# A new order for the first batch of an attention-and-FFN kernel: k first, split roles for the k features, first FFN units 128 columns wide

## The chip, the cores and the metric

The kernel runs on one core of a Trainium2 chip. The metric is the time of one execution in microseconds (us); most executions of one kernel agree within 0.3%. In the text PE is the tensor engine, DVE is VectorE, ACT is ScalarE, POOL is GpSimd, SP is the engine whose queue issues most DMAs. The granted clock of PE is the share of its full clock that the profile shows as allowed.

## The reference

A linear attention with cosine and sine position weights, then a gated FFN. Cut to what matters:

```python
# q, k, v: (8, 8, 576, 64) = batch, heads, sequence, head size
r = maximum(x, 0); phi(x) = concat([r * cos_w, r * sin_w], axis=-1)
kv  = einsum('bhsf,bhsd->bhfd', phi(k), v)        # 128 x 64 per head
z   = sum(phi(k), axis=2)
out = einsum('bhsf,bhfd->bhsd', phi(q), kv) / (einsum('bhsf,bhf->bhs', phi(q), z) + 1e-6)
x   = out as (4608 tokens, 512)
y   = (gelu(x @ w_gate) * (x @ w_val)) @ w_out    # 512 -> 1536 -> 512
```

Nearly all the work is the FFN's matmuls. The attention of later batches is spread among them; only the first batch's attention has nothing to hide behind. That stretch, up to the first FFN matmul, is called the prologue here.

## The kernel before

Loads and the first batch, with cuts marked. One token row group is `(pair m, j)`: four head pairs, nine j, 64 numbers each. `kp` and `qp` are phi(k) and phi(q), `vx` is v in bf16 with a column of ones (so that z comes out of the same matmul as kv). `qT` is phi(q) transposed; the numerators are the matmuls of `qT` with kv; `den` and `rec` are the denominators and their reciprocals, `x_sb` the attention's output and `xT` its transpose; `gel` and `hT` are the gelu of the gate and its product with the value; `jt` counts the twelve blocks of 128 hidden units. Banks are parts of PSUM, the memory that PE writes.

```python
    load(nc.sync, "qf", q, 0, ((0, 2),), 0, 4)      # q, j 0 to 3 ("the q slice")
    load(nc.scalar, "qf", q, 0, ((2, 2),), 0, 4)
    load(nc.sync, "kf", k, 0, ((0, 2),))
    load(nc.scalar, "kf", k, 0, ((2, 2),))
    load(nc.sync, "vf", v, 0, ((0, 2),))
    load(nc.sync, "vf", v, 0, ((2, 1),))
    # ... tables of cos and sin
    load(nc.scalar, "vf", v, 0, ((3, 1),))
    load(nc.scalar, "qf", q, 0, ((0, NP),), 4, R)   # q, j 4 to 8 ("the rest of q")
    # ...
    def prep(name, b, j0, j1, m=0, n=NP, parts=(0, 1)):       # DVE, four pairs per op
        for j in range(j0, j1):
            for part in parts:
                nc.vector.tensor_scalar(dst[:, m:m + n, j, ...], src[:, m:m + n, j], 0.0,
                                        (cos_t, sin_t)[part][:, j:j + 1], op0=ALU.max, op1=ALU.mult)
    # prep_wide: DVE scalar_tensor_tensor, one pair, many j; prep_act: ACT Relu with a scale
    def kv_unit(b, groups=1):
        ps = psum[:, 4:6]                                     # both groups in the same banks
        # ...
        for g in range(groups):
            # 36 matmuls, then
            nc.scalar.copy(kv[:, g * per:(g + 1) * per], psv[:, g * per:(g + 1) * per])
    # ...
    nc.gpsimd.tensor_copy(probe, staged["kf", 0][:, 2, 0:1])  # POOL waits for k,
    load_w(0, 2)                                              # then issues all weight loads
    for jt in range(2, 8, 3):                                 # (on POOL's queue; they cast
        load_w(jt, 3)                                         # float32 to bf16 on the way)
    # ... loads of batch 1 and of w_out
    for m in range(NP):
        for part in range(2):
            prep_wide("qp", 0, 0, 4, m, part)
    turn_q_pe(0, 0, 4, (0, 1), (None, None))
    prep_act("kp", 0, 1, 0, 2)
    prep_wide("kp", 0, 0, R, 0, 0)
    prep_wide("kp", 0, 0, R, 1, 0)
    cast_v(0, 0, 2, nc.vector.tensor_copy)
    prep_act("kp", 0, 1, 2, 2)
    # ... the other two pairs the same way
    turn_copies(0, 0, 4, (0, 1), (nc.scalar.copy, nc.vector.tensor_copy))
    keep_warm(50)                  # 128x128 matmuls whose result nobody reads
    kv_unit(0, 2)
    keep_warm(8)
    nm_unit(0, 0)                  # numerators; then on DVE den, rec, x_sb = numerator * rec
    nm_unit(0, 1, 0)
    keep_warm(8)
    xt_unit(0, 0)                  # PE transposes, ACT copy to xT
    keep_warm(8)
    xt_unit(0, 1, 7)
    prep("qp", 0, 4, 6)
    prep("qp", 0, 6, 8)
    for jt in range(8):
        gv_unit(0, 256, jt)        # FFN: gate and value of 128 hidden units, 256 tokens
        # ... narrow turns of q (both in bank 7), numerators and transposes of tiles 2 to 4
```

Of the kernel before, what the change touches and what calls it, by code (L numbers as in the profile page):

```python
# [9 lines left out]
FP32 = mybir.dt.float32  # L10
# [6 lines left out]
def kernel(  # L17
# [14 lines left out]
    nc = tc.nc  # L32

    B, H, S, D = q.shape
# [5 lines left out]
    NP = H // 2  # L40
    R = S // 64
# [5 lines left out]
    consts = ctx.enter_context(tc.tile_pool(name="consts", bufs=1))  # L47
# [8 lines left out]


    psum = psp.tile([128, 8, BLK], FP32)
    ring = [0, 1, 2, 3]

    def next_bank():
        ring.append(ring.pop(0))
# [6 lines left out]
    staged = {}  # L69

    def load(eng, name, src, b, cuts=((0, NP),), j0=0, j1=R):
        if (name, b) not in staged:
            staged[name, b] = inp.tile(
                [128, NP, R * D], FP32, name=name, bufs=2 if name == "qf" else 1
            )
        js = slice(j0 * D, j1 * D)
        for m, n in cuts:
            eng.dma_start(
                out=staged[name, b][:, m:m + n, js], in_=rows(src, b)[:, m:m + n, js]
            )  # L80
# [8 lines left out]
    def load_w(jt0, n):  # L89
        sl = slice(jt0 * 128, (jt0 + n) * 128)  # L90
        nc.gpsimd.dma_start(out=wg_sb[:, :, sl], in_=wg_r[:, :, sl])
        nc.gpsimd.dma_start(out=wv_sb[:, :, sl], in_=wv_r[:, :, sl])
# [3 lines left out]



    load(nc.sync, "qf", q, 0, ((0, 2),), 0, 4)
    load(nc.scalar, "qf", q, 0, ((2, 2),), 0, 4)  # L100
    load(nc.sync, "kf", k, 0, ((0, 2),))
    load(nc.scalar, "kf", k, 0, ((2, 2),))
    load(nc.sync, "vf", v, 0, ((0, 2),))
    load(nc.sync, "vf", v, 0, ((2, 1),))

    pos_i = consts.tile([128, R], mybir.dt.int32)
    nc.gpsimd.iota(pos_i, pattern=[[1, R]], base=0, channel_multiplier=R)
# [2 lines left out]
    ident = consts.tile([128, 128], BF16)  # L110
# [10 lines left out]
    cos_t = consts.tile([128, R], FP32)  # L121
    nc.scalar.activation(sin_t, pos_f, AF.Sin, scale=th_scale)
    nc.scalar.activation(cos_t, pos_f, AF.Sin, scale=-th_scale, bias=half_pi)
    load(nc.scalar, "vf", v, 0, ((3, 1),))
    load(nc.scalar, "qf", q, 0, ((0, NP),), 4, R)
    warm = consts.tile([128, 1], FP32)
    nc.scalar.activation(warm, half_pi, AF.Gelu)
    vx_tiles = []
# [13 lines left out]
    def prep(name, b, j0, j1, m=0, n=NP, parts=(0, 1)):  # L142

        dst = phi_tile(name, b)
        src = staged[name[0] + "f", b].rearrange("p m (j d) -> p m j d", j=R)
        for j in range(j0, j1):
            for part in parts:
                nc.vector.tensor_scalar(  # L148
                    dst[:, m:m + n, j, part * D:(part + 1) * D],
                    src[:, m:m + n, j],  # L150
                    0.0,
                    (cos_t, sin_t)[part][:, j:j + 1],
                    op0=ALU.max,
                    op1=ALU.mult,
                )

    def prep_wide(name, b, j0, j1, m, part):
        nc.vector.scalar_tensor_tensor(  # L158
            phi_tile(name, b)[:, m, j0:j1, part * D:(part + 1) * D],
            staged[name[0] + "f", b][:, m].rearrange("p (j d) -> p j d", j=R)[:, j0:j1],  # L160
            0.0,
            (cos_t, sin_t)[part][:, j0:j1, None].to_broadcast([128, j1 - j0, D]),
            op0=ALU.max,
            op1=ALU.mult,
        )

    def prep_act(name, b, part, m=0, n=NP, j0=0, j1=R):

        dst = phi_tile(name, b)
        src = staged[name[0] + "f", b].rearrange("p m (j d) -> p m j d", j=R)  # L170
        for j in range(j0, j1):
            nc.scalar.activation(
                dst[:, m:m + n, j, part * D:(part + 1) * D],
                src[:, m:m + n, j],
                AF.Relu,
                scale=(cos_t, sin_t)[part][:, j:j + 1],
            )

    def cast_v(b, m=0, n=NP, copy=nc.gpsimd.tensor_copy):
        copy(  # L180
            vx_tiles[b % 2][:, m:m + n, :, 0:D],
            staged["vf", b][:, m:m + n].rearrange("p m (j d) -> p m j d", j=R),
        )
# [10 lines left out]
    def turn_q_pe(b, j0, n, banks=(4, 5), engines=None):  # L194

        if engines is None:
            engines = (nc.scalar.copy, nc.vector.tensor_copy)
        per = NP // len(banks)
        views = [
            psum[:, g].bitcast(BF16)[:, 0:per * n * 128].rearrange(  # L200
                "f (m j c) -> f m j c", m=per, j=n
            )
            for g in banks
        ]
        for m in range(NP):
            for j in range(n):
                nc.tensor.transpose(  # L207
                    out=views[m // per][:, m % per, j],
                    in_=phi["qp", b][:, m, j0 + j, :],
                    identity=ident,  # L210
                )
        if engines[0] is not None:
            turn_copies(b, j0, n, banks, engines)

    def turn_copies(b, j0, n, banks, engines):
        per = NP // len(banks)
        for g, copy in enumerate(engines):
            ps = psum[:, banks[g]].bitcast(BF16)[:, 0:per * n * 128].rearrange(
                "f (m j c) -> f m j c", m=per, j=n
            )  # L220
            for i in range(2):
                copy(
                    qt_tile(b)[i][
                        :, g * per:(g + 1) * per, j0 * 64:(j0 + n) * 64
                    ].rearrange("f m (j p) -> f m j p", p=64),
                    ps[:, :, :, i * 64:(i + 1) * 64],
                )

    def turn_q_narrow(b, j0, n, copy=nc.scalar.copy):
        turn_q_pe(b, j0, n, (7,), (copy,))  # L230

    def turn_q(b, pair0, n):
        qt_tile(b)
# [8 lines left out]

    kv_sb = {}

    def kv_unit(b, groups=1):
        kp, vx = phi["kp", b], vx_tiles[b % 2]
        ps = psum[:, 4:6]
        kv = attn2.tile([128, NP, 2, D + 1], BF16, name="kv_sb")
        psv = ps[:, :, 0:NP * (D + 1)].rearrange("p i (m d) -> p m i d", m=NP)
        per = NP // groups  # L250
        for g in range(groups):
            for pair in range(g * per, (g + 1) * per):
                for j in range(R):
                    for i in range(2):
                        rr = slice(64 * i, 64 * i + 64)
                        nc.tensor.matmul(  # L256
                            psv[:, pair, i],
                            lhsT=kp[rr, pair, j, :],
                            rhs=vx[rr, pair, j, :],
                            start=(j == 0),  # L260
                            stop=(j == R - 1),
                        )
            nc.scalar.copy(kv[:, g * per:(g + 1) * per], psv[:, g * per:(g + 1) * per])
        kv_sb[b] = kv

    bt = {}
# [117 lines left out]
            load(nc.sync, "qf", q, b + 1)  # L384


    probe = consts.tile([128, 1], FP32)
    nc.gpsimd.tensor_copy(probe, staged["kf", 0][:, 2, 0:1])
    load_w(0, 2)
    for jt in range(2, 8, 3):  # L390
        load_w(jt, 3)
    load(nc.gpsimd, "qf", q, 1)
# [4 lines left out]
    load_wo(0, 6)  # L397
    load_wo(6, 6)

    for m in range(NP):  # L400
        for part in range(2):
            prep_wide("qp", 0, 0, 4, m, part)
    turn_q_pe(0, 0, 4, (0, 1), (None, None))
    prep_act("kp", 0, 1, 0, 2)
    prep_wide("kp", 0, 0, R, 0, 0)
    prep_wide("kp", 0, 0, R, 1, 0)
    cast_v(0, 0, 2, nc.vector.tensor_copy)
    prep_act("kp", 0, 1, 2, 2)
    prep_wide("kp", 0, 0, R, 2, 0)
    prep_wide("kp", 0, 0, R, 3, 0)  # L410
    cast_v(0, 2, 1, nc.vector.tensor_copy)
    cast_v(0, 3, 1, nc.vector.tensor_copy)
    turn_copies(0, 0, 4, (0, 1), (nc.scalar.copy, nc.vector.tensor_copy))

    def keep_warm(n):
        for _ in range(n):
            nc.tensor.matmul(
                psum[:, 7, 0:128], lhsT=ident, rhs=ident, start=True, stop=True
            )

    keep_warm(50)
    kv_unit(0, 2)
    keep_warm(8)
    nm_unit(0, 0)
    nm_unit(0, 1, 0)
# [1 line left out]
    xt_unit(0, 0)  # L427
    keep_warm(8)
    xt_unit(0, 1, 7)
    prep("qp", 0, 4, 6)  # L430
    prep("qp", 0, 6, 8)
    for jt in range(8):
        gv_unit(0, 256, jt)
        if jt == 0:
            turn_q_narrow(0, 4, 2)
            prep("qp", 0, 8, R)
        if jt == 1:
            turn_q_narrow(0, 6, 2)
        if jt == 2:
            nm_unit(0, 2)  # L440
        if jt == 3:
            turn_q_narrow(0, 8, 1)
        if jt == 4:
            nm_unit(0, 3)
            xt_unit(0, 2)
        if jt == 6:
            xt_unit(0, 3)
        if jt == 7:
            nm_unit(0, 4)
# [39 lines left out]

    ring[:] = [2, 3]  # L490
    o_step(0, 0)
    kv_unit(1, 2)
    load(nc.gpsimd, "kf", k, 2)
    load(nc.gpsimd, "vf", v, 2)
    fill(4)
# [51 lines left out]
    for blk in range(2, 9):  # L547
        b = blk + 1
# [24 lines left out]
    for half, copy, eng in (  # L573
# [4 lines left out]
        for jt in range(JT):  # L578
            nc.tensor.matmul(  # L579
                psum[:, 4 + half, 0:256],  # L580
                lhsT=hT[8][:, jt, 384:512],
                rhs=wo_sb[:, jt, cs],
                start=(jt == 0),
                stop=(jt == JT - 1),
# [33 lines left out]
```

## Time and profile before

| | before |
|---|---|
| time, median of the 3 runs made before the change | 345.82 us (345.78 to 345.93) |
| PE busy, share of the span | 94% |
| first FFN matmul starts at | 19.29 us |
| k-v groups of batch 1 start at | 46.36 us |

The page's first part, busy time of each engine in us (share of the span) and number of instructions:

```profile
span 344.4 us, 6826 instructions
...
PE 324.5 (94%) x2700; PEld 180.9 (53%) x2738; DVE 192.4 (56%) x533; ACT 139.3 (40%) x281; POOL 30.5 (9%) x51
```

PE is nearly always busy, so time can only be won where PE waits. That is the prologue, and a few waits later. The chain of waits, followed back from the last instruction, in order of time (start us, us, what), up to the first FFN matmul:

```profile
10.23 1.04 DVE vx_119 L180
11.27 1.32 DVE kp L158 x2
12.59 1.32 DVE vx_119 L180 x2
13.92 0.34 DVE qT_194 L222
14.26 0.75 PE psum L256 x36
...
15.99 0.18 DVE den L283
...
16.43 0.69 DVE x_sb L285
...
17.47 0.70 DVE x_sb L285
...
18.65 0.59 ACT xT L319
...
19.29 1.03 PE psum L334 x8
```

Read it as a sentence: v's DMA lands at 10.2 us, DVE casts v and makes the cosine half of phi(k) in turns until 13.9, then a copy of q's transposes, the second k-v group runs on PE (14.26), numerators, two rounds of den, rec, x_sb on DVE (15.99 to 18.17), transposes, ACT's copy of xT, FFN at 19.29. (L256 are the k-v matmuls, L285 x_sb, L319 the xT copy, L334 the FFN's gate and value matmuls.)

The chain puts the second k-v group's wait down to a copy of q's transposes, which that group does not read. v's last cast had ended at 13.91; what ended just before 14.26, at 14.19, is ACT's copy of the first group out of the same banks (start us, us, engine, line, operation, output<-input):

```profile
13.82 0.37 ACT L263 CAST kv_sb<-psum 128x260 bf16<-128x260 f32 x1
```

So the shared banks are the likelier cause here too.

Waits between 36 and 50 us (who waited for whom: us in total, times, longest):

```profile
PE psum L256 <- ACT kv_sb L263: 0.5, 1, 0.5
```

This is batch 1's second k-v group, which waits for ACT's copy of the first out of the same banks.

### The profile page before, as it was taken

The page shows a single profiled execution, that of the slowest core. Times are in us where ns is not written, and L with a number is a line of the kernel's source. Part 1 is how long each engine was busy: PE and PEld are TensorE (multiplying, and loading weights), DVE is VectorE, ACT ScalarE, POOL GpSimd, SP SyncE. Part 2 cuts the span into 40 slices and gives each one's busy share as a digit, 9 for nine tenths or more (in the row PEclk, how much of TensorE's full clock was granted, in tenths as well). Part 3 has the DMA queues.
Part 4 walks back from the last instruction along what each step waited for, and adds up shares of the span by engine and source line. Part 5 has one row for each costly group of instructions (what it writes and reads, how often), then busy time and mean ns, then how long its engine had stood idle before and what let it go on. Part 6 is the DMA issues. An engine that isn't in the chain of part 4 may idle for free.

```text
span 344.4 us, 6826 instructions
## 1 busy us (share of the span) xinstructions
PE 324.5 (94%) x2700; PEld 180.9 (53%) x2738; DVE 192.4 (56%) x533; ACT 139.3 (40%) x281; POOL 30.5 (9%) x51
## 2 busy tenths in 40 slices
PE   3889998989899999999999999999999999999994
PEld 2778656755445554555455545554555444444443
DVE  5677865994792598258825882588355222322300
ACT  4667955533423443334324433343244333223221
POOL 1831022000200200020002000200000000000000
PEclk9999999999999999999999999999999999999999
DMA  7999984019569807990789079606711111211124
GB/s 285 260 273 305 240 296 163 2 36 371 207 86 237 317 4 107 227 340 0 99 203 370 3 86 216 236 0 92 139 32 33 30 30 38 50 35 30 32 62 91
DMA packets 47888, 48.81 MB, mean 142 GB/s; under 512 B 25200, under 2 KB 33136, under 8 KB 47856
## 3 DMA queue, kind: packets, MB, share of 16 engines
q1 hardware_dynamic: 38000, 34.64, 39.7%
q0 software_dynamic: 8480, 11.80, 14.4%
q10 hardware_dynamic: 1376, 1.93, 1.6%
q8 instruction: 21, 0.34, 0.4%
q14 instruction: 11, 0.09, 0.1%
HBM read 37.75 MB, written 9.44 MB: 137 GB/s over the span
## 4 chain that ended last, share of the span: by engine, by line
PE 88%; DVE 6%; DMA 2%; ACT 1%; issue 1%; SPq 0%; DVEq 0%; ACTq 0%
PE psum L334 52%; PE psum L365 25%; PE psum L256 3%; PE psum L272 3%; PE psum L312 2%; DMA vf<-in_v_dram 2%; DVE kp L148 1%; PE psum L207 1%; DVE x_sb L285 1%; DVE hT L345 1%; PE psum L579 1%; DVE vx_119 L180 1%; ACT xT L319 0%; DVE kp L158 0%; ACT gel L342 0%
## 5 line engine op out<-in xcount | busy, mean ns | idle before, releaser
L345 DVE TENSOR_TENSOR hT<-gel,psum 128x512 bf16<-128x512 f32 (+4 forms) x132 | 77.5, 590 | 127.3 <-PE psum L334 115.1
L342 ACT ACTIVATE gel<-psum 128x512 f32<-128x512 f32 (+4 forms) x132 | 68.5, 520 | 127.7 <-PE psum L334 121.6
L334 PE MATMUL psum<-xT,wg_sb 128*128 128x512 bf16 (+4 forms) x515 | 113.6, 339 | 2.4 <-ACT xT L319 1.4
L334 PE MATMUL psum<-xT,wv_sb 128*128 128x512 bf16 (+4 forms) x516 | 113.2, 339 | 0.6
L365 PE MATMUL psum<-wo_sb,hT 128*128 128x512 bf16 x407 | 104.3, 379 | 1.2 <-issue 0.8
L334 PEld LDWEIGHTS <-wg_sb 128*128 128x128 bf16 x528 | 48.4, 98 | 47.1 <-issue 2.1
L334 PEld LDWEIGHTS <-wv_sb 128*128 128x128 bf16 x528 | 49.0, 98 | 45.4
L365 PEld LDWEIGHTS <-hT 128*128 128x128 bf16 x420 | 38.7, 98 | 39.0
L319 ACT COPY xT<-psum 128x512 bf16<-128x512 bf16 (+1 forms) x44 | 21.9, 508 | 24.4 <-PE psum L312 24.3
L374 ACT COPY o_sb<-psum 128x512 f32<-128x512 f32 x35 | 20.5, 585 | 27.7 <-PE psum L365 26.6
L285 DVE TENSOR_TENSOR x_sb<-psum,rec 128x512 bf16<-128x512 f32 x40 | 27.7, 691 | 1.4
L148 DVE TENSOR_SCALAR qp<-qf,cos_t 128x256 bf16<-128x256 f32 x68 | 23.6, 347 | 0.0
L148 DVE TENSOR_SCALAR kp<-kf,cos_t 128x256 bf16<-128x256 f32 x63 | 21.7, 349 | 0.0
L148 DVE TENSOR_SCALAR qp<-qf,sin_t 128x256 bf16<-128x256 f32 x59 | 20.5, 347 | 0.0
L148 DVE TENSOR_SCALAR kp<-kf,sin_t 128x256 bf16<-128x256 f32 x57 | 20.0, 350 | 0.0
L312 PE MATMUL psum<-ident,x_sb 128*128 128x128 bf16 x160 | 15.5, 219 | 1.7 <-DVE x_sb L285 1.5
L180 POOL CAST vx_121<-vf 128x576 bf16<-128x576 f32 x12 | 7.5, 669 | 96.0 <-DMA vf<-in_v_dram 65.1
L207 PE MATMUL psum<-ident,qp 128*128 128x128 bf16 x108 | 9.2, 232 | 6.3 <-DVE qp L158 5.2
L180 POOL CAST vx_119<-vf 128x576 bf16<-128x576 f32 (+1 forms) x10 | 7.2, 765 | 65.6 <-DMA vf<-in_v_dram 65.6
L256 PEld LDWEIGHTS <-kp 64*128 64x128 bf16 x576 | 10.1, 95 | 5.4 <-issue 3.4
L312 PEld LDWEIGHTS <-x_sb 128*128 128x128 bf16 x160 | 10.0, 97 | 4.7 <-DVE x_sb L285 3.5
L207 PEld LDWEIGHTS <-qp 128*128 128x128 bf16 x108 | 7.3, 103 | 8.3 <-DVE qp L158 6.1
(88 smaller groups left out, 163.5 us busy)
## 6 DMA issues: line engine op xcount, KB each, us to landing
out_dram<-o_sb SPq DMA_DIRECT2D x70, 128.0 KB, 2.4
qf<-in_q_dram SPq DMA_DIRECT2D x5, 1152.0 KB, 11.6
kf<-in_k_dram SPq DMA_DIRECT2D x5, 1152.0 KB, 5.9
vf<-in_v_dram SPq DMA_DIRECT2D x5, 1152.0 KB, 9.2
qf<-in_q_dram POOLq DMA_DIRECT2D x2, 1152.0 KB, 16.3
kf<-in_k_dram POOLq DMA_DIRECT2D x2, 1152.0 KB, 11.4
vf<-in_v_dram POOLq DMA_DIRECT2D x2, 1152.0 KB, 11.8
wo_sb<-in_moe_w_out_dram POOLq DMA_DIRECT2D x2, 768.0 KB, 17.8
```

Of the source, the lines that this page charges most:

```text
L148: nc.vector.tensor_scalar(dst[:, m:m + n, j, part * D:(part + 1) * D], src[:, m:m + n, j], 0.0, (cos_t, sin_t)[part][:, j:j + 1], op0=ALU.max,
L180: copy(vx_tiles[b % 2][:, m:m + n, :, 0:D], staged["vf", b][:, m:m + n].rearrange("p m (j d) -> p m j d", j=R),)
L207: nc.tensor.transpose(out=views[m // per][:, m % per, j], in_=phi["qp", b][:, m, j0 + j, :], identity=ident,)
L256: nc.tensor.matmul(psv[:, pair, i], lhsT=kp[rr, pair, j, :], rhs=vx[rr, pair, j, :], start=(j == 0), stop=(j == R - 1),)
L285: nc.vector.tensor_tensor(x, nm[:, :, :, 0:D], rec[:, :, :, None].to_broadcast([128, 2, 4, D]), op=ALU.mult,)
L312: nc.tensor.transpose(out=ps[:, ct, :], in_=x[:, ct * 128:(ct + 1) * 128], identity=ident)
L319: nc.scalar.copy(xT_block(blk)[:, :, c:c + m], ps[:, :, o:o + m])
L334: nc.tensor.matmul(ps[:, 0:n], lhsT=w[:, ct, js], rhs=xt[:, ct, cc:cc + n], start=(ct == 0), stop=(ct == CT - 1),)
L342: nc.scalar.activation(gel[:, 0:n], g_ps[:, 0:n], AF.Gelu)
L345: nc.vector.tensor_mul(hT[blk][:, jt, cc:cc + n], gel[:, 0:n], v_ps[:, 0:n])
L365: nc.tensor.matmul(o_ps[i], lhsT=hT[blk][:, jt, tt * 128:(tt + 1) * 128], rhs=wo_sb[:, jt, :], start=(jt == 0), stop=(jt == JT - 1),)
L374: nc.scalar.copy(o_sb, o_ps.pop(i))
```

## The change

Its intent: start DVE and ACT on k as soon as k can be there, let both halves of phi(k) be made side by side in four-pair ops (cosines on DVE, sines on ACT), move the warm-up matmuls to where PE is idle anyway, hold back the weights (a first gate on q, a second on v's cast), prepare q's j 4 to 7 before den, and let the first FFN units of 128 tokens start when only tile 0 is ready. Both k-v groups get banks of their own, in batches 0 and 1, and so does the second narrow turn of q (`ring` is the order in which PSUM banks are handed out). The core of the diff:

```diff
-    ring = [0, 1, 2, 3]
+    ring = [2, 3, 0, 1]
+    load(nc.sync, "kf", k, 0, ((0, 2),))
+    load(nc.scalar, "kf", k, 0, ((2, 2),))
     load(nc.sync, "qf", q, 0, ((0, 2),), 0, 4)
     load(nc.scalar, "qf", q, 0, ((2, 2),), 0, 4)
-    load(nc.sync, "kf", k, 0, ((0, 2),))
-    load(nc.scalar, "kf", k, 0, ((2, 2),))
     load(nc.sync, "vf", v, 0, ((0, 2),))
-    load(nc.sync, "vf", v, 0, ((2, 1),))
 ...
-    load(nc.scalar, "vf", v, 0, ((3, 1),))
-    load(nc.scalar, "qf", q, 0, ((0, NP),), 4, R)
+    load(nc.scalar, "vf", v, 0, ((2, 2),))
+    load(nc.sync, "qf", q, 0, ((0, NP),), 4, R)
 ...
-    def kv_unit(b, groups=1):
+    def kv_unit(b, banks=(4,)):
 ...
+        for g, bank in enumerate(banks):
+            psv = psum[:, bank:bank + 2, 0:per * (D + 1)].rearrange(...)
 ...
-    probe = consts.tile([128, 1], FP32)
-    nc.gpsimd.tensor_copy(probe, staged["kf", 0][:, 2, 0:1])
+    probe = consts.tile([128, 2], FP32)
+    nc.gpsimd.tensor_copy(probe[:, 0:1], staged["qf", 0][:, 0, 0:1])
     load_w(0, 2)
+    prep_act("kp", 0, 1)
+    prep("kp", 0, 0, R, parts=(0,))
+    for m in range(NP):
+        for part in range(2):
+            prep_wide("qp", 0, 0, 4, m, part)
+    keep_warm(80)
+    turn_q_pe(0, 0, 4, (0, 1), (None, None))
+    cast_v(0, 0, 2, nc.scalar.copy)
+    cast_v(0, 2, 2, nc.vector.tensor_copy)
+    turn_copies(0, 0, 4, (0, 1), (nc.scalar.copy, nc.vector.tensor_copy))
+    nc.gpsimd.tensor_copy(probe[:, 1:2], vx_tiles[0][:, 2, 0, 0:1])
     for jt in range(2, 8, 3):
         load_w(jt, 3)
 ...   (the old first batch, shown above, removed)
-    keep_warm(50)
-    kv_unit(0, 2)
+    prep("qp", 0, 4, 8)
+    keep_warm(6)
+    kv_unit(0, (4, 2))
 ...
-    prep("qp", 0, 4, 6)
-    prep("qp", 0, 6, 8)
+    gv_unit(0, 128, 0)
+    gv_unit(0, 128, 1)
+    gv_unit(128, 128, 0)
     for jt in range(8):
-        gv_unit(0, 256, jt)
+        if jt == 1:
+            gv_unit(128, 128, 1)
+        elif jt > 1:
+            gv_unit(0, 256, jt)
 ...
-            turn_q_narrow(0, 6, 2)
+            turn_q_narrow(0, 6, 2, 6)
 ...
-    kv_unit(1, 2)
+    kv_unit(1, (4, 0))
```

More of the change, by code (lines that the diff above doesn't have):

```diff
@@ L227, in turn_copies, with turn_q_narrow @@
                 )
-    def turn_q_narrow(b, j0, n, copy=nc.scalar.copy):
-        turn_q_pe(b, j0, n, (7,), (copy,))
+    def turn_q_narrow(b, j0, n, bank=7, copy=nc.scalar.copy):
+        turn_q_pe(b, j0, n, (bank,), (copy,))
     def turn_q(b, pair0, n):
@@ L243 @@
     kv_sb = {}
-    def kv_unit(b, groups=1):
+    def kv_unit(b, banks=(4,)):
         kp, vx = phi["kp", b], vx_tiles[b % 2]
-        ps = psum[:, 4:6]
         kv = attn2.tile([128, NP, 2, D + 1], BF16, name="kv_sb")
-        psv = ps[:, :, 0:NP * (D + 1)].rearrange("p i (m d) -> p m i d", m=NP)
-        per = NP // groups
-        for g in range(groups):
-            for pair in range(g * per, (g + 1) * per):
+        per = NP // len(banks)
+        for g, bank in enumerate(banks):
+            psv = psum[:, bank:bank + 2, 0:per * (D + 1)].rearrange(
+                "p i (m d) -> p m i d", m=per
+            )
+            for m in range(per):
                 for j in range(R):
@@ L256, in kv_unit @@
                         nc.tensor.matmul(
-                            psv[:, pair, i],
-                            lhsT=kp[rr, pair, j, :],
-                            rhs=vx[rr, pair, j, :],
+                            psv[:, m, i],
+                            lhsT=kp[rr, g * per + m, j, :],
+                            rhs=vx[rr, g * per + m, j, :],
                             start=(j == 0),
@@ L262, in kv_unit @@
                         )
-            nc.scalar.copy(kv[:, g * per:(g + 1) * per], psv[:, g * per:(g + 1) * per])
+            nc.scalar.copy(kv[:, g * per:(g + 1) * per], psv)
         kv_sb[b] = kv
@@ L384, in load_batch, with keep_warm @@
             load(nc.sync, "qf", q, b + 1)
-    probe = consts.tile([128, 1], FP32)
-    nc.gpsimd.tensor_copy(probe, staged["kf", 0][:, 2, 0:1])
-    load_w(0, 2)
+    def keep_warm(n):
+        for _ in range(n):
+            nc.tensor.matmul(
+                psum[:, 7, 0:128], lhsT=ident, rhs=ident, start=True, stop=True
+            )
+    probe = consts.tile([128, 2], FP32)
+    nc.gpsimd.tensor_copy(probe[:, 0:1], staged["qf", 0][:, 0, 0:1])
+    load_w(0, 2)
+    prep_act("kp", 0, 1)
[9 more added lines that the diff above has]
+    nc.gpsimd.tensor_copy(probe[:, 1:2], vx_tiles[0][:, 2, 0, 0:1])
     for jt in range(2, 8, 3):
@@ L398 @@
     load_wo(6, 6)
-    for m in range(NP):
-        for part in range(2):
-            prep_wide("qp", 0, 0, 4, m, part)
-    turn_q_pe(0, 0, 4, (0, 1), (None, None))
-    prep_act("kp", 0, 1, 0, 2)
-    prep_wide("kp", 0, 0, R, 0, 0)
-    prep_wide("kp", 0, 0, R, 1, 0)
-    cast_v(0, 0, 2, nc.vector.tensor_copy)
-    prep_act("kp", 0, 1, 2, 2)
-    prep_wide("kp", 0, 0, R, 2, 0)
-    prep_wide("kp", 0, 0, R, 3, 0)
-    cast_v(0, 2, 1, nc.vector.tensor_copy)
-    cast_v(0, 3, 1, nc.vector.tensor_copy)
-    turn_copies(0, 0, 4, (0, 1), (nc.scalar.copy, nc.vector.tensor_copy))
-    def keep_warm(n):
-        for _ in range(n):
-            nc.tensor.matmul(
-                psum[:, 7, 0:128], lhsT=ident, rhs=ident, start=True, stop=True
-            )
-    keep_warm(50)
-    kv_unit(0, 2)
+    prep("qp", 0, 4, 8)
+    keep_warm(6)
+    kv_unit(0, (4, 2))
     keep_warm(8)
```

## The prediction

> **What bounds it now.** By the page's busy table the tensor engine (PE) is busy 94% of the 344.4 us span; the chain that ended last is 88% PE. From 19.29 us, the first FFN matmul, PE has almost no gaps (5.00 of 5 us busy in 25:30 and 30:35 by the stage table). So the change can earn only (a) an earlier first FFN matmul and (b) the few later waits it touches.
>
> **The prologue before.** The chain in order of time: v lands (10.2), VectorE (DVE) casts v and makes k cosines until 13.9, qT copy, second k-v group 14.26, numerators, den/reciprocal/x_sb (15.99 to 18.17), transposes, xT copy, FFN at 19.29. ScalarE (ACT) does k sines in eighteen 128x128 ops, 7.60 to 12.98.
>
> **Costed, from the trace's durations.**
> - Load order. The Trainium skill, "DMA: Bandwidth & Descriptors" (Issuing engines are not separate DMA queues), says all queues share the same 16 engines; the trace agrees (382 to 403 GB/s in each microsecond from 3 to 10). So only the order moves: k should land about 6.4 (7.6 to 8.0 before), the q slice 7.7, v about 10.7, the rest of q about 13.
> - ACT k sines in nine 128x256 ops: about 0.41 us apart, 3.8 us instead of 5.4, done about 10.3. ACT then casts half of v (1.15 us).
> - DVE becomes the prologue's chain: 9 k cosines (0.26 apart, 2.4 us), 8 wide q ops (2.7), v cast (1.04), two qT copies (0.75): free about 13.4. Then comes the q preparation for j 4 to 8, moved ahead of den (2.1 us, to 15.6), although PE could deliver numerators about 15.1: this costs about 0.5. x_sb of tile 1 ends about 17.8 (18.17 before).
> - First FFN units at 128 columns need only tile 0's xT, so they fill the 0.67 us wait for the second xT copy: first FFN matmul about 18.1 instead of 19.29. Four half units cost about 0.25 us more PE than two whole ones. The second narrow q turn in its own bank saves 0.29 us. Worth about 1.4 us by unit jt=2.
> - Weights go the other way. jt>=2 is issued only after DVE's v cast (about 12.9; 9.9 before). Cast loads from GpSimd took about 3 us from issue to first packet (8.28 to 11.3) and run near 200 GB/s as written; they should start about 15.8 against 14.0 before. The w_val slab for jt 5 to 7, landed about 23.3 before and first used at 26.4, would land about 25.2, where the faster PE wants it about 24.9. I expect a small stall here: net prologue gain 1.0 to 1.4.
> - Batch 1's k-v groups in own banks: removes the 0.45 us between the groups (47.13 to 47.58), all on the chain.
> - The warm-up matmuls (PE first, 80) are off the path.
>
> Sum: -1.15 - 0.45, about 1.6 us.
>
> **Prediction: 344.2 us, 343.2 to 345.4 eight times in ten.** Faster by over 2%: 0.01; within 2%: 0.98; slower by over 2%: 0.01.
>
> **What would show it.** Timeline: first FFN matmul (wg_sb) at 17.7 to 18.6; DVE with no idle from about 6.5 to 17.8; den starting right after the q preparation, not after PE; k sines done near 10.3. Waits: no PE wait on the qT copy near 20 nor between batch 1's k-v groups; possibly a PE wait for wv_sb near 25. From 60 us on, the same stages as before, shifted.
>
> **What would make it wrong.** Weights later than estimated (a PE stall of 1 us or more on wg_sb/wv_sb between 20 and 26): the gain vanishes, about 345.5. PE's clock falling while it idles between the warm-ups and the k-v groups: up to 1 us lost. The rest of q landing after 13.5: den later by as much. If q preparation does not hold den up, 0.5 us more is gained.

## The result, and the profile after

| | before | after |
|---|---|---|
| time, median of 4 runs | 345.8 us (345.76 to 345.93) | 344.44 us (344.42 to 344.63) |
| PE busy, share of the span | 94% | 95% |
| first FFN matmul starts at | 19.29 us | 18.12 us |
| gate matmuls of unit jt=2 start at | 22.37 us | 20.80 us |
| k-v groups of batch 1 start at | 46.36 us | 45.04 us |

The ratio is 0.9961 (95% interval 0.9944 to 0.9979). Ratios are the mean time of one kernel's fast runs over that of the other's of the same rounds, so not quite the ratio of the medians. The medians differ by 1.36 us. The two profiled runs differ by 1.74 (346.18 and 344.44), because the profiled run of the kernel before was 0.4 us above its median.

The page's busy times and the chain of waits of the kernel after, to be read against those of before:

```profile
span 342.7 us, 6928 instructions
...
PE 325.5 (95%) x2752; PEld 182.5 (53%) x2790; DVE 191.8 (56%) x538; ACT 139.0 (41%) x275; POOL 30.3 (9%) x52
```

```profile
6.23 2.63 DVE kp L147 x9
8.86 2.69 DVE qp L157 x8
...
11.60 0.40 PE psum L206 x4
12.00 0.34 PE psum L390 x6
12.33 1.27 PE psum L257 x72
...
14.15 0.53 PE psum L273 x16
14.68 1.07 DVE qp L147 x3
15.75 0.09 DVE den L284
...
16.10 0.69 DVE x_sb L286
...
17.14 0.70 DVE x_sb L286
...
18.28 1.34 PE psum L335 x24
```

The chain no longer starts with v but with k (landed at 6.2 us, before 7.5 to 8.0). From there DVE has no gap worth the name until the second x_sb ends at 17.8: nine k cosines, eight wide q ops, the v cast, two qT copies, the q preparation for j 4 to 7, den. Note the line `DVE qp L147 x3` ahead of den: the numerators were done (14.15 + 0.53), and den waited for DVE to finish the q preparation. (From 11.60 to 14.68 the list goes through PE, but DVE was busy all that time too.) No xT copy stands between the last transposes and the FFN: the first units need tile 0 only. The chain's first FFN piece is at 18.28; the first FFN matmul itself stands earlier in the timeline:

```profile
18.12 0.39 PE L335 MATMUL psum<-xT,wg_sb 128*128 128x128 bf16 x4
```

The same waits between 36 and 50 us hold no line of PE waiting for `kv_sb` any more. The chain there (start us, us, what) goes straight through both groups:

```profile
45.04 1.42 PE psum L257 x72
...
46.49 0.39 ACT kv_sb L264
...
46.89 0.23 ACT gel L343
```

One thing in the timeline of the kernel after (start us, us, engine, line, operation, output<-input) was not expected. These are POOL's DMA issues and DVE's q preparation in the same stretch:

```profile
13.14 0.76 POOL L92 DMA_DIRECT2D wv_sb<-in_moe_w_val_dram  x1
13.16 0.33 DVE L147 TENSOR_SCALAR qp<-qf,sin_t 128x256 bf16<-128x256 f32 x1
13.42 0.59 DVE L147 TENSOR_SCALAR qp<-qf,cos_t 128x256 bf16<-128x256 f32 x1
...
13.87 0.77 POOL L91 DMA_DIRECT2D wg_sb<-in_moe_w_gate_dram  x1
13.93 0.34 DVE L147 TENSOR_SCALAR qp<-qf,sin_t 128x256 bf16<-128x256 f32 x1
...
14.19 0.57 DVE L147 TENSOR_SCALAR qp<-qf,cos_t 128x256 bf16<-128x256 f32 x1
```

The eight ops of one shape (12.80 to 15.67) take 0.44, 0.33, 0.59, 0.34, 0.57, 0.34, 0.56 and 0.33 us; there are four POOL issues (12.40, 13.14, 13.87, 14.60), and one long op for each. But the long ones are also all cosines. Experiment e10 below tests that.

### The profile page after: what moved, and what is told of

Same layout as the page of the kernel before. It is cut to its first block, busy times and chain, and to the rows that moved or that the text cites. A ratio compares the mean times of both kernels' runs of the same rounds, so it can differ in the third digit from the quotient of the medians.

```text
span 342.7 us, 6928 instructions
## 1 busy us (share of the span) xinstructions
PE 325.5 (95%) x2752; PEld 182.5 (53%) x2790; DVE 191.8 (56%) x538; ACT 139.0 (41%) x275; POOL 30.3 (9%) x52
## 3 DMA queue, kind: packets, MB, share of 16 engines
q0 software_dynamic: 8480, 11.80, 14.6%
q10 hardware_dynamic: 976, 1.57, 1.3%
## 4 chain that ended last, share of the span: by engine, by line
PE 87%; DVE 7%; DMA 2%; issue 1%; ACT 1%; DVEq 0%; ACTq 0%
PE psum L335 52%; PE psum L366 26%; PE psum L257 3%; PE psum L273 3%; PE psum L313 2%; DVE kp L147 2%; DMA kf<-in_k_dram 2%; DVE x_sb L286 1%; PE psum L206 1%; DVE hT L346 1%; DVE qp L157 1%; PE psum L582 1%; ACT gel L343 1%; DVE rec L285 0%; DVE qp L147 0%
## 5 line engine op out<-in xcount | busy, mean ns | idle before, releaser
L346 DVE TENSOR_TENSOR hT<-gel,psum 128x512 bf16<-128x512 f32 (+5 forms) x134 | 77.7, 583 | 127.3 <-PE psum L335 115.1
L343 ACT ACTIVATE gel<-psum 128x512 f32<-128x512 f32 (+5 forms) x134 | 68.8, 515 | 126.7 <-PE psum L335 120.9
L335 PE MATMUL psum<-xT,wg_sb 128*128 128x512 bf16 (+5 forms) x523 | 114.0, 337 | 1.8 <-ACT xT L320 0.7
L335 PE MATMUL psum<-xT,wv_sb 128*128 128x512 bf16 (+5 forms) x524 | 113.5, 337 | 0.6
L147 DVE TENSOR_SCALAR kp<-kf,cos_t 128x256 bf16<-128x256 f32 x72 | 24.2, 349 | 4.6 <-DMA kf<-in_k_dram 4.6
L147 DVE TENSOR_SCALAR qp<-qf,cos_t 128x256 bf16<-128x256 f32 x68 | 24.5, 361 | 0.0
L147 DVE TENSOR_SCALAR qp<-qf,sin_t 128x256 bf16<-128x256 f32 x59 | 20.4, 345 | 0.0
L147 DVE TENSOR_SCALAR kp<-kf,sin_t 128x256 bf16<-128x256 f32 x57 | 19.8, 347 | 0.0
L206 PE MATMUL psum<-ident,qp 128*128 128x128 bf16 x108 | 8.3, 219 | 2.9 <-DVE qp L157 2.2
L390 PE MATMUL psum<-ident 128*128 128x128 bf16 x110 | 9.0, 253 | 1.6 <-POOL ident masks.py:199 1.6
## 6 DMA issues: line engine op xcount, KB each, us to landing
kf<-in_k_dram POOLq DMA_DIRECT2D x2, 1152.0 KB, 11.2
wo_sb<-in_moe_w_out_dram POOLq DMA_DIRECT2D x2, 768.0 KB, 18.1
```

Of the source, the lines that this page charges most:

```text
L147: nc.vector.tensor_scalar(dst[:, m:m + n, j, part * D:(part + 1) * D], src[:, m:m + n, j], 0.0, (cos_t, sin_t)[part][:, j:j + 1], op0=ALU.max,
L206: nc.tensor.transpose(out=views[m // per][:, m % per, j], in_=phi["qp", b][:, m, j0 + j, :], identity=ident,)
L335: nc.tensor.matmul(ps[:, 0:n], lhsT=w[:, ct, js], rhs=xt[:, ct, cc:cc + n], start=(ct == 0), stop=(ct == CT - 1),)
L343: nc.scalar.activation(gel[:, 0:n], g_ps[:, 0:n], AF.Gelu)
L346: nc.vector.tensor_mul(hT[blk][:, jt, cc:cc + n], gel[:, 0:n], v_ps[:, 0:n])
```

## The experiments

Twelve kernels were run, five or six timed runs each, all correct. Times are medians; the ratio is against the kernel before in the same rounds (the kernel after has 0.9961). e1 to e4 and e9 to e11 ran on one chip, e5 to e8 and e12 on another; they stand here by subject.

**e1: the first two FFN units whole again.**

```diff
-    gv_unit(0, 128, 0)
-    gv_unit(0, 128, 1)
-    gv_unit(128, 128, 0)
     for jt in range(8):
-        if jt == 1:
-            gv_unit(128, 128, 1)
-        elif jt > 1:
-            gv_unit(0, 256, jt)
+        gv_unit(0, 256, jt)
```

> The changed kernel with its first two FFN units whole again (256 columns, waiting for both xT copies). Theory: the 128-column units fill the wait for the second xT copy; undone, the tensor engine waits about 0.65 us there again and saves about 0.05 us of matmul time: 344.44 + 0.4 to 0.6, about 344.95. Rival (the halves cost as much tensor time as the wait they fill): no difference, 344.4 to 344.5.

Measured: 345.19 us (344.96 to 345.45), ratio 0.9981; the span of its profiled run is 343.2 us against 342.7. The chain goes through ACT's xT copy again:

```profile
17.75 0.41 PE psum L313 x4
...
18.18 0.59 ACT xT L320
...
18.82 1.03 PE psum L335 x8
```

So the half units earn 0.5 (spans) to 0.75 us (medians). The theory holds; the rival falls.

**e2: batch 1's two k-v groups in the same banks again.**

```diff
-    kv_unit(1, (4, 0))
+    kv_unit(1, (4, 4))
```

> The changed kernel with batch 1's two k-v groups in the same banks again. Theory: the second group waits for ScalarE's copy of the first (0.45 us before), all of it on the chain: about 344.9, and a tensor engine wait of about 0.45 us between the two groups near 45.8. Rival (the freed time is given back at the next wait, ScalarE's copy and gelu behind it): under 0.1 us, 344.4 to 344.55.

Measured: 344.92 us (344.91 to 345.04), ratio 0.9975. The 0.45 us is there again, and the end is 0.48 us later, so nothing of it is given back:

```profile
45.13 0.77 PE psum L257 x36
...
45.92 0.38 ACT kv_sb L264
...
46.35 0.76 PE psum L257 x36
```

**e3: the q slice loaded ahead of k again.**

```diff
-    load(nc.sync, "kf", k, 0, ((0, 2),))
-    load(nc.scalar, "kf", k, 0, ((2, 2),))
     load(nc.sync, "qf", q, 0, ((0, 2),), 0, 4)
     load(nc.scalar, "qf", q, 0, ((2, 2),), 0, 4)
+    load(nc.sync, "kf", k, 0, ((0, 2),))
+    load(nc.scalar, "kf", k, 0, ((2, 2),))
```

> The changed kernel with the q slice loaded ahead of k again, nothing else. Theory: the prologue is one VectorE chain that starts when k lands (6.2 us); k then lands about 7.5, and everything up to the first FFN matmul moves by as much: first FFN matmul about 19.4 instead of 18.12, time about 345.6. Rival (v's landing still sets the start, as it did before): v lands at the same time, 344.4 to 344.6.

Measured: 346.34 us (346.21 to 346.56), ratio 1.0015: slower than the kernel before. k cosines start at 7.98 instead of 6.23, the first FFN matmuls on the chain at 20.12 instead of 18.28. The theory holds, with 1.9 us where 1.2 was expected. Most of the rest is k itself, which let DVE start at 7.98 and not at about 7.5. PE's clock fell to half between 13 and 16 us in this run's stage table (0.78, 0.50, 0.50), so that the 72 k-v matmuls took 2.10 us on the chain instead of 1.27 and den (17.50) waited for PE; but DVE had ended its q preparation only at 17.31, so this cost no more than about 0.2 us.

**e9: the kernel before with k loaded first, nothing else.** (The same two pairs of lines exchanged, in the kernel before.)

> The kernel before with only the load order changed: k ahead of the q slice. Theory (load order and compute order only pay together: VectorE still works on q first and now waits until about 7.7 for it, and k cosines, v casts and qT copies follow): the first FFN matmul moves from 19.29 to about 20.5 to 21, time 346.8 to 347.6. Rival (v's landing sets the start, k early helps anyway): 345.2 to 345.9.

Measured: 348.16 us (347.88 to 348.56), ratio 1.0065, 2.3 us slower than the kernel before. Here is a part of its chain:

```profile
7.68 2.78 DVE qp L158 x8
...
11.12 3.69 PE psum L417 x50
14.81 0.70 PE psum L256 x36
```

DVE started on q at 7.68, and then the 50 warm-up matmuls (L417), which stand behind q's transposes in PE's order, came onto the chain and held the k-v groups up until 14.81. That term was missing in the expectation. It is not the whole loss: DVE's last cast of v ended at 15.13, and the second k-v group ran at 15.97, so by an estimate from these two the warm-ups cost at most 0.8 us. The first FFN matmul came at 21.01, the upper edge of what was expected; the time lies above its range. e3 and e9 together: the new compute order with q first is 0.56 us slower than the kernel before (1.9 slower than the kernel after), the new load order alone is 2.3 us slower. Each loses alone and they win only together, with the warm-ups moved to the front of PE's order (a move that no run tests by itself in the kernel before).

**e4: den ahead of the q preparation.**

```diff
-    prep("qp", 0, 4, 8)
     keep_warm(6)
 ...
     nm_unit(0, 1, 0)
+    prep("qp", 0, 4, 8)
     keep_warm(8)
     xt_unit(0, 0)
```

> The changed kernel with the q preparation for j 4 to 8 after the two x_sb instead of ahead of den. Theory: it holds den up by about 1.2 us (numerators done at about 14.4, den at 15.67); den then starts near 14.4, the first FFN matmul near 16.9 and the time falls by 0.6 to 1.2, to 343.2 to 343.8, unless the weights of jt 2 to 7 come too late (then waits for wg_sb/wv_sb show near 20 to 25). Rival (the preparation is needed as early as it stands, by the narrow turns): given back at the turns and the first hT, 344.3 to 344.8.

Measured: runs of 344.28, 344.38, 345.24, 345.43, 345.47 and 345.53 us, ratio 0.9978. The first half of the theory came true: den at 14.53, first FFN matmul at 16.99. The second half did not. The profiled run (344.38) shows where it went: the q preparation now stands ahead of the first products hT, which began at 19.42; ACT's third gelu waited 1.43 us for a buffer that hT frees, ACT's copies of q's turns followed late, and at 24.02 (the numerators of tile 3) PE was only 0.14 us ahead of the kernel after (24.16). A lead of 1.13 us was given back within 7 us:

```profile
14.53 0.18 DVE den L284
...
24.02 0.42 PE psum L273 x8
```

The rival is right for this run and the one at 344.28. The other four lie about 1 us higher, above the rival's range too. No trace of them was kept, but the record has a lower mean granted clock for them (0.993 to 0.995, against 0.997 and 0.999).

**e5: the k sines in eighteen two-pair ops again.**

```diff
-    prep_act("kp", 0, 1)
+    prep_act("kp", 0, 1, 0, 2)
+    prep_act("kp", 0, 1, 2, 2)
```

> The changed kernel with the k sines in eighteen two-pair ScalarE ops again. Theory (VectorE is the prologue's chain): sines end near 11.6 instead of 9.92, the v cast and qT copies on ScalarE and the k-v groups move about 1.0 us, numerators end near 15.4, still ahead of den at 15.67: time within 0.15 us of 344.44. Rival (ScalarE's sines gate the k-v groups): 345.2 to 345.6.

Measured: 344.64 us (344.39 to 344.75), ratio 0.9958, no difference from the kernel after. The sines took 5.37 us instead of 3.70 and ended at 11.2 instead of 9.9, and the chain in the profile is the same. The four-pair sines, named in the change's intent, are worth nothing by themselves: ACT is not the chain.

**e6: without the second gate.**

```diff
-    nc.gpsimd.tensor_copy(probe[:, 1:2], vx_tiles[0][:, 2, 0, 0:1])
```

> The changed kernel without the gate on v ahead of the weights of jt 2 and up, which then issue from 9.5 us. Theory (GpSimd's weight packets do not flow before the hardware queues run dry, at about 11.5 in both kernels): v lands as before at about 10.6, the first FFN matmul stays at 18.1, time 344.3 to 344.5. Rival (the gate keeps weights from v's bandwidth): v lands 0.5 to 1.5 us later and the time rises by 0.3 to 1.

Measured: runs of 344.42, 344.42, 344.6, 344.74, 344.85 and 346.0 us, ratio 0.9966. v lands as before (ACT's cast starts at 10.68, 10.59 in the kernel after), so the gate does not protect v. With POOL still issuing, DVE's v cast took 0.88 us instead of 0.75, but only three of the q preparation's ops were long then, and it ended at 15.82 instead of 15.75. In the profiled run (344.85) PE's clock fell to 0.50 in 12:15, and den waited for PE until 15.96. The time is about the expected one, but e8 shows that the reason given for it is wrong.

**e8: with neither gate.**

```diff
-    nc.gpsimd.tensor_copy(probe[:, 0:1], staged["qf", 0][:, 0, 0:1])
 ...
-    nc.gpsimd.tensor_copy(probe[:, 1:2], vx_tiles[0][:, 2, 0, 0:1])
```

> The changed kernel with neither gate: all GpSimd loads issue from about 2 us. Theory (software packets wait until the hardware queues run dry): first software packet near 11.4 as before, k at 6.2, same time, 344.3 to 344.6. Rival 1 (the 3 to 3.6 us seen between issue and first packet are latency): packets from about 5 us on, q and v late by 1 to 4 us, time 345.5 to 348. In between: they share from 5 us and v lands near 13.

Measured: four runs of 345.85 to 346.31 us, two of about 349.0; ratio 1.003, interval 0.9999 to 1.006. POOL issued its first load at 1.61. Between 5 and 6 us two software packets moved, the first at 5.96, and from 6 to 7 us the queues read (queue, kind: packets, MB, share of 16 engines):

```profile
q1 hardware_dynamic: 130, 0.13, 44.8%
q10 hardware_dynamic: 131, 0.13, 37.7%
q0 software_dynamic: 96, 0.05, 35.4%
```

q0 is POOL's queue, q1 and q10 are SP's and ACT's. So software packets do run beside busy hardware queues, from 7 to 8 us as an equal third party by packets (99 beside 99 and 103). They only come late: 4.4 us after the first issue here, 3.0 us in the kernel before (8.28 to 11.28), 3.6 us in the kernel after (7.88 to 11.53); what sets the length is open. That they came just as the hardware queues ran dry in those two was not the cause; my theory of e6 and e8 falls, and rival 1 (latency, then sharing) is right. What they cost: v at 11.7 (ACT's cast) and the rest of q not before 15.1, which then heads the chain. The first gate is worth about 1.5 us (346.17 against 344.67 in e6, which differs by this gate alone). Why two runs took 349 us was not seen in a trace.

**e7: without the 80 early warm-ups.**

```diff
-    keep_warm(80)
```

> The changed kernel without the 80 early warm-up matmuls. Theory (they end at 8.2, and what sets the start is VectorE): the k-v groups and numerators may run at the slow rate, at most about 1 us later, which the wait for den hides: 344.4 to 344.8. Rival (the clock must be raised early): the tensor engine is still slow at the first FFN units, 345 to 346.5.

Measured: four runs of 344.42 to 344.53 us and one, the profiled one, of 345.09; ratio 0.9959. In that run the k-v matmuls took 2.10 us, den came at 16.33, and the FFN ran at full rate from its start. The stage table reads a granted clock of 1.00 for those matmuls, but the trace's list of clock changes begins only at 16.07 in this run (at 5.85 in the kernel after): before the first entry a table's 1.00 says nothing. So the 80 warm-ups are worth nothing in four runs and 0.6 us in one of five. What the tensor clock does in the other four runs no trace shows.

**e10: POOL quiet while DVE prepares q.**

```diff
     load_w(0, 2)
+    load_w(2, 3)
 ...
-    nc.gpsimd.tensor_copy(probe[:, 1:2], vx_tiles[0][:, 2, 0, 0:1])
-    for jt in range(2, 8, 3):
-        load_w(jt, 3)
+    prep("qp", 0, 4, 8)                       # moved up a few lines; same place in DVE's order
+    nc.gpsimd.tensor_copy(probe[:, 1:2], phi["qp", 0][:, 0, 7, 64:65])
+    load_w(5, 3)
```

> The changed kernel with the weights of jt 2 to 4 issued right behind those of jt 0 and 1 (from 7.9 to 11), and the rest only after the q preparation for j 4 to 8. Theory (each GpSimd DMA issue holds up one VectorE op by about 0.23 us; in the changed kernel four such issues fall into the q preparation): those eight ops take 2.1 us instead of 2.87, den starts near 14.95 instead of 15.67, first FFN matmul near 17.4, time 343.6 to 344.0 where the k-v groups run at the fast rate (with them slow, den waits for the numerators near 16.0 and nothing is gained). Rival (VectorE's slower ops come from something else, such as other engines' SBUF traffic): the ops stay at 0.56 us, time 344.3 to 344.6.

Measured: runs of 343.61, 343.64, 344.55, 344.68 and 344.77 us, ratio 0.9949. The same eight ops, with POOL idle from 11.0 to 15.0:

```profile
12.77 0.34 DVE L147 TENSOR_SCALAR qp<-qf,cos_t 128x256 bf16<-128x256 f32 x1
...
14.34 0.35 DVE L147 TENSOR_SCALAR qp<-qf,cos_t 128x256 bf16<-128x256 f32 x1
...
14.60 0.35 DVE L147 TENSOR_SCALAR qp<-qf,sin_t 128x256 bf16<-128x256 f32 x1
...
15.13 0.75 POOL L91 DMA_DIRECT2D wg_sb<-in_moe_w_gate_dram  x1
```

All eight, cosines too, take 0.34 to 0.35 us and end at 14.95; the rival falls. (e8 shows the same unasked: there the preparation ran from 15.13 on with POOL idle, and all eight ops took 0.35 us.) POOL's issues between 9.5 and 11 did no harm, because DVE's wide q ops (scalar_tensor_tensor) stayed at 0.41 us beside them. But den in this profiled run (344.68) came at 15.90, released by PE. The stage table (stretch, us, PE busy and count, PEld, DVE, ACT, POOL, granted clock, DMA share, GB/s) shows why, for the kernel after and then for e10:

```profile
11.00:12.00 1.00, 0.72 (x11) 0.55 (x12) 1.00 (x3) 1.00 (x2) 0.00 (x0) 1.00 1.20 299
12.00:13.00 1.00, 1.00 (x52) 0.90 (x51) 1.00 (x4) 0.71 (x2) 0.72 (x2) 1.00 1.45 197
```

```profile
11.00:12.00 1.00, 0.73 (x11) 0.56 (x11) 1.00 (x3) 1.00 (x2) 0.00 (x0) 0.96 1.16 310
12.00:13.00 1.00, 1.00 (x26) 0.80 (x25) 1.00 (x4) 0.76 (x2) 0.00 (x0) 0.50 1.46 198
```

The granted clock (third number from the end) fell to 0.50 just as the k-v groups began, and they took 2.10 us instead of 1.27. PE had been idle from 7.9 to 9.6 and about half idle from there to 11.5. The same program can come out either way: the two runs at 343.6 fit the expectation for the fast rate, the three near 344.7 fit that for the slow one. In the kernel after most of this would be hidden, since den waits for DVE until 15.67 anyway; not all of it, for with the groups at 2.10 us den came at 15.96 in e6 and at 16.33 in e7.

**e11: e10 without idle time on PE.** Ninety-six warm-ups instead of 80, and four more after each four transposes of q.

> e10 with 96 early warm-up matmuls instead of 80 and 4 more after each four q transposes, so that the tensor engine has no idle time from 1.6 to 12. Theory (the engine falls back to its slow rate in some executions because it is nearly idle from 8.2 to 11.6, which makes the spread of the runs): k-v groups take about 1.3 us in the profile, runs within 0.2 us of each other, about 343.7. Rival (the spread has another cause): runs spread by 0.3 to 1 us as in the runs so far.

Measured: runs of 343.74, 344.57, 344.62, 344.66, 344.67 and 346.12 us, ratio 0.9966. The clock stayed at 1.00 in the profiled run (344.57) and the k-v groups took 1.3 us, yet it was no faster: this time DVE waited 0.84 us for the rest of q, which landed at 13.7, since its last packets came in one by one among POOL's weight packets up to 13.2. The theory explains at most one of two causes of the spread.

**e12: e11 with the rest of q on two queues.**

```diff
-    load(nc.sync, "qf", q, 0, ((0, NP),), 4, R)
+    load(nc.sync, "qf", q, 0, ((0, 2),), 4, R)
+    load(nc.scalar, "qf", q, 0, ((2, 2),), 4, R)
```

> e11 with the rest of q in two halves, one on each hardware queue, instead of all of it on one. Theory (in e11's profile the clock stayed up, but the last packets of the rest of q came in among GpSimd's weight packets until 13.5, so that the q preparation waited 0.84 us for it; two queues hold two shares of three against the weights instead of one of two): the rest of q lands before 12.8, den starts near 14.9, granted clock 1.00 in 12:15; most runs 343.5 to 343.8. Rival (which engine gets behind is chance, and the split does not change it): q lands near 13.5 in most runs and they stay at 344.5 to 344.7 as in e11.

Measured: runs of 343.65, 343.66, 343.75, 344.9, 346.26 and 346.61 us, ratio 0.9961. Half the runs are where the theory wants them. The profiled one is not (346.26): the rest of q came even later (DVE waited 1.23 us, until 14.08), PE then sat idle from 15.3 to 17.4, and its clock fell to a mean of 0.76 in 18:20, in the first FFN units. So the split does not cure it. What decides when the last packets of q come is open. e10 to e12 reach 343.6 us in six of their seventeen runs, counting 343.75 and lower, but none does so reliably, so no version is shown to beat the kernel after.

When the clock falls can be worked out from the traces kept, though no run was made for it. Each trace lists when the granted clock changed. After its first rise (5.85 in the kernel after, 5.09 in e10) it changed only after whole multiples of 3.41 us, and each fall before the kernel's end lasted 3.41 us. In the 3.41 us before such a fall PE was busy for 1.37 us (e6), 1.47 (e12), 1.54 (e10) and 1.58 (e3). In every other such stretch after the first rise, up to about 19 us and in all fourteen traces, it was busy for 1.79 us or more (the least in e11), and the clock stayed. The first rise comes at another time in each run, so the same idle time can fall into one stretch or be divided over two. That fits the two branches, and so does the mean granted clock of each run: in e4, e6 and e10 the runs below 344.5 us have 0.997 to 0.999, those above 0.992 to 0.995. It is not proved for them, since no trace of a run of e10 at 343.6 us was kept.

## Why the prediction was right

The measured 344.44 us lies in the range, 0.24 from the point. Step by step:

- *Load order: "k should land about 6.4, the q slice 7.7, v about 10.7".* 6.2, 7.66 (POOL's gate on q) and 10.59. Right. The Trainium skill's point in "DMA: Bandwidth & Descriptors" (Issuing engines are not separate DMA queues) carried this: the trace has 380 to 392 GB/s in 8:9 and 9:10 with the new order, as with the old.
- *"DVE becomes the prologue's chain."* Right: the chain shows it, e3 (k later, all later) and e5 (ACT slower, nothing later) confirm it.
- *"free about 13.4 ... q preparation (2.1 us, to 15.6)".* The sum was right (den at 15.67), two of its terms were not, and they cancelled, which was luck. DVE was free at 12.80; about half of these 0.6 us is its v cast, which took 0.75 us, not the 1.04 read from the trace before, where POOL had been issuing at the same time. The q preparation took 2.87 us, not 2.1, since POOL now issued beside that. It is one effect, seen from both sides (e10).
- *"this costs about 0.5".* Den did wait about 1.1 us after the numerators (14.6), twice what was allowed for, but that is not what it costs: e4 removed the wait and in its profiled run kept only 0.14 us of it at 24 us.
- *First FFN matmul at 18.1; half units worth the xT copy less 0.25 us.* 18.12; e1 gives 0.5 to 0.75 us, more than the 0.42 forecast, because the four half units took 1.78 us of PE where the two whole ones took 1.75: 0.03 us more and not 0.25. PE's wait of 0.29 us on the narrow turn's copy (before 21.93) is gone, as forecast.
- *"Worth about 1.4 us by unit jt=2."* 1.57 us (22.37 to 20.80).
- *"should start about 15.8 ... I expect a small stall here".* Wrong. I took the 3 us between issue and first packet for a cost of every load. The weights of jt 2 and up were issued at 12.40 while POOL's queue still had those of jt 0 and 1 to move, and their first packets (768 bytes each, against 512 for the first slabs) came at 14.21, 1.8 us after the issue. Software packets took 145% of the engines' span in 12:13 and again in 13:14 (over 100% since packets overlap); in place of a gap there is a dip to 91% and 82% between 14.5 and 15.0. The slab of `w_val` for jt 5 to 7 landed about 24.1 and not 25.2, and no PE wait for weights shows between 20 and 26. The lead of 1.57 us did shrink to 1.32 by 45 us, as "net 1.0 to 1.4" said, but for another reason: PE waited at 24.16 for tile 2's x_sb, because ACT, busy with four qT copies from 20.1 to 22.3, gave its gelu late. The range of the net gain was met without its reason.
- *"removes the 0.45 us between the groups ... all on the chain".* Right: e2 measures 0.48.
- *"The warm-up matmuls are off the path."* Right for most runs (e7), but it hid two things: left where they were, they came onto the chain when k was loaded first (e9), and a falling clock is only hidden as long as den waits for DVE (e10).
- *Sum: -1.15 - 0.45.* 1.36 us by medians, 1.74 between the profiled runs. By medians the part without batch 1's groups is then about 0.9 us (1.36 less the 0.48 of e2), a little under the forecast; the 1.32 of the profiles probably holds the 0.4 us by which the profiled run of the kernel before was slow.

## What to carry to other kernels

Before moving work earlier, list for the new order which engine's queue each step stands in and what it waits for; a load order and a compute order that fit each other can both lose alone (e3, e9), and a start that is earlier can be given back by the next in-order queue (e4). Durations read from a trace carry their neighbours with them: a DVE op timed beside POOL's DMA issues is not the same op without them, so look at what else ran before using its time in a sum. When an effect is below 0.5%, read each run: a mean over two branches of the same program (here 343.6 and 344.6) says little about either.

## What the Trainium skill lacked or had wrong

- "SBUF — State Buffer", Who interferes with whom, says that a 2-port DVE instruction and GpSimd block each other for the whole instruction. The trace agrees that ops lengthen where the two overlap. But the size is neither op's whole time: each POOL DMA issue of about 0.76 us held up one DVE op by about 0.23 us (0.57 against 0.34; one long op per issue), and only tensor_scalar ops and casts lengthened, not scalar_tensor_tensor with float32 inputs (0.41 us with and without). A figure per DMA issue would let one cost it ahead.
- "DMA: Bandwidth & Descriptors", Specifications, gives about 1 us to the first byte for DMAs from GpSimd. Casting loads here took 3.0 to 4.4 us from the start of the first issue to their first packets (8.28 to 11.28, 7.88 to 11.53, 1.61 to 5.96), while the hardware queues were full. With packets of POOL's own queue still moving it was 1.8 us (12.40 to 14.21).
- "TensorE: Matmul & The Clock Gate", What's actually happening, says that the window is free-running and the rate halves after idle time. The traces agree: the rate was 0.50 in 12:15 of e10 and 1.00 in the kernel after, the first rise came anywhere from 4.98 (e6) to 16.07 us (e7), and each fall before the kernel's end lasted 3.41 us. What the page lacks is how busy PE has to be. Here the rate fell after stretches of 3.41 us with 1.37 to 1.58 us of PE work (e3, e6, e10, e12), and stayed after those with 1.79 us or more.
- No page tells how long the last packets of a hardware queue can be delayed by a full software queue beside it: in e11 and e12 the last few of the rest of q came up to 1.3 to 1.4 us after the others (11.91 to 13.19 in e11, 11.90 to 13.29 in e12).
